# Linear attention and a cos-gated MLP on one core: three subtractions of a row maximum moved from VectorE to GpSimd, with a new order of steps

## The chip, the core and the metric

The kernel runs on one core of a Trainium2 chip. A core has a matrix engine (PE), a vector engine (DVE, also VectorE), a scalar engine (ACT), a general engine (POOL, also GpSimd) and an engine that here only issues transfers (SP); each works through its own list of instructions in order and waits on semaphores for the others. The metric is the device time of one execution in microseconds (us).

## The reference

Eight batches of eight heads, sequence S = 576, head size D = 64, all in float32.

```python
q_s = softmax(q, axis=-1)          # over D, with the row maximum subtracted first
k_s = softmax(k, axis=2)           # over S, with the column maximum subtracted first
kv  = einsum("bhsd,bhse->bhde", k_s, v)
x   = einsum("bhsd,bhde->bhse", q_s, kv)     # to 4608 x 512 (tokens x heads*D)
h   = x @ w_in                     # 512 x 2048
out = (h * cos(h)) @ w_out         # 2048 x 512
```

The subtraction that this document is about is `q - max(q, axis=-1)`, a step of the softmax of q.

## The kernel before, in words

The heads of a batch are taken two at a time; the four pairs of a batch are numbered 0 to 3. A batch's q lies in two tiles of 128 rows by 9 blocks by 128 columns (1152 columns), one for pairs 0 and 1 and one for pairs 2 and 3. Names in the trace: `q`, `qload` (q as loaded; in batch 0, pairs 2 and 3), `qm` (row maxima), `qs` (row sums), `k`, `mt` and `m` (column maxima of k over halves, over all partitions), `kv`, `r`, `kvw` (kv in PSUM, the inverse of its row sums, kv normalised), `qt` (q transposed), `x_False` and `x_True` (the rounded part of q kv, and its remainder), `w_i`, `w_o` (weights of the MLP), `h`, `acc`.

For one tile of q the steps are, each a call of `plan.add` in `q_steps`: the row maximum (`q_max`, DVE, L865), the subtraction (`q_sub`, DVE, L869), the exponential (`q_exp`, ACT, L880 and L883), the row sum (`q_sum`, DVE, L888), its inverse (`q_inv`, DVE, L892 and L893) and the normalisation (`q_norm`, DVE, L896). For k: `k_max` and its two followers (DVE, L698, L703, L707), `k_all`, the maximum over all 128 partitions (POOL, an all-reduce, L713), `k_sub` (DVE, L720), `k_exp` (ACT, L726). Then PE takes `kv` (L775), DVE makes `kvw` (L792, L795, L802), PE transposes q (`qt`, L1013) and multiplies (`x_False`, `x_True`, L1062). In batch 0 each pair of k goes through these steps by itself, in later batches two pairs together. The MLP runs in units of 512 columns of tokens; its first product is `h` at L1233, its second `acc` at L1509. The weights come as raw 512 KB blocks and are split into a rounded part and a remainder by ACT (L502, L507, L528) and DVE (L511, L517, L537), block by block, before the unit that needs them.

All of this is first written down as a list of steps. `plan.add(engine, us, fn, reads, writes)` appends one; the `us` there is a planning number and is not used when the kernel is built. The list `ORDER`, written out as step numbers, then says in which order the steps are issued, and so in which order each engine meets them:

```python
steps = plan.order(ORDER)
for i in steps:
    if plan.steps[i][2]:
        plan.steps[i][2]()
```

Nothing reorders them later: an engine that waits for one step holds up everything behind it on the same engine.

Of the kernel before, what the change touches and what calls it, by code (L numbers as in the profile page):

```python
# [49 lines left out]
    KVD=((0, 0), (0, 1), (0, 2), (0, 3), (1, 0), (1, 1), (1, 2), (1, 3)),  # L50
    SB=3,
# [220 lines left out]
def linear_attention_then_cos_gated_mlp(  # L272
# [203 lines left out]
    def convert(ws, f):  # L476
# [55 lines left out]
        def lo():  # L532
            t = T["wp", ws, f]
            for i, w in enumerate(ws):
                c, h, l = T["wc", ws, f][:, i], t[:, i, 0].bitcast(F32), t[:, i, 1]
                if w == "i":
                    nc.vector.tensor_sub(l, c, h)  # L537
                else:
                    nc.vector.tensor_sub(split(l), dealt(c), split(h))
# [1225 lines left out]
```

## Time and profile before

| | us |
|---|---|
| median of three runs | 812.35 |
| the three runs | 810.69, 812.35, 813.06 |
| the profiled execution, whole | 811.02 |
| its span, first to last instruction | 809.2 |
| PE busy in the span | 789.3 |
| DVE busy | 647.3 |
| ACT busy | 545.9 |
| POOL busy | 42.7 |

The span is what the trace shows; the execution adds 1.8 us around it. A busy time is the sum of an engine's instructions, without its waits. The granted clock of PE was 0.999 of full speed.

### The profile page before, as it was taken

What the parts mean: (1) busy time and instruction counts of PE and PEld (TensorE: products, weight loads), DVE (VectorE), ACT (ScalarE), POOL (GpSimd) and SP (SyncE); (2) the same over time, 40 slices, a digit from 0 to 9 for tenths busy, and PEclk for the clock granted to TensorE, in tenths of its full rate; (3) what the DMA queues carried; (4) which work ended last, traced back from release to release, by engine and by line L of the source; (5) the groups of instructions that cost most, each with busy time, mean ns of one, the idle gap of its engine ahead of it and who ended that gap; (6) DMA issues with size and microseconds to landing.
All of it is one profiled execution on the core that took longest, in us unless ns stands there. A gap on an engine that the chain in (4) does not pass through costs nothing.

```text
span 809.2 us, 14405 instructions
## 1 busy us (share of the span) xinstructions
PE 789.3 (98%) x5172; PEld 707.2 (87%) x5172; DVE 647.3 (80%) x1140; ACT 545.9 (67%) x1004; POOL 42.7 (5%) x153
## 2 busy tenths in 40 slices
PE   3899999999999999999999999999999999999997
PEld 2766888888888889999999999999999999999996
DVE  9999999889789898999787879887797656654444
ACT  4999888955656558767877678676666565555441
POOL 1200100000100010002000110003000000000000
PEclk9999999999999999999999999999999999999999
DMA  7877833458665688889889988897977676546621
GB/s 233 274 220 214 246 117 122 149 154 238 188 194 164 145 255 263 242 259 261 235 273 258 274 273 253 227 286 248 296 203 215 235 255 245 190 174 222 220 80 53
DMA packets 202967, 175.02 MB, mean 216 GB/s; under 512 B 111120, under 2 KB 173072, under 8 KB 202896
## 3 DMA queue, kind: packets, MB, share of 16 engines
q1 hardware_dynamic: 202576, 173.58, 71.0%
q8 instruction: 41, 0.67, 0.3%
q10 hardware_dynamic: 320, 0.52, 0.2%
q14 instruction: 30, 0.25, 0.1%
HBM read 139.72 MB, written 34.34 MB: 215 GB/s over the span
## 4 chain that ended last, share of the span: by engine, by line
PE 97%; SPq 2%; DMA 1%; issue 0%; DVE 0%
PE acc L1509 44%; PE h L1362 20%; PE h L1233 16%; PE pb L1362 8%; PE x_False L1062 3%; PE acc L1502 3%; PE kv L775 2%; DMA v<-in_v_dram 1%; PE x_True L1062 0%; PE qt L1013 0%; SPq L632 0%; SPq L583 0%; SPq L574 0%; SPq L613 0%; SPq L663 0%
## 5 line engine op out<-in xcount | busy, mean ns | idle before, releaser
L1239 ACT ACTIVATE kt<-h 128x512 int32<-128x512 f32 x144 | 85.8, 596 | 112.0 <-PE h L1362 82.8
L1509 PE MATMUL acc<-w_o,ghi 128*128 128x512 f32 x456 | 136.4, 381 | 0.0
L1243 DVE SCALAR_TENSOR_TENSOR kt<-kt,h 128x512 f32<-128x512 int32 x144 | 97.1, 681 | 36.2 <-ACT kt L1239 35.3
L1249 ACT ACTIVATE kt<-kt 128x512 f32<-128x512 f32 x144 | 89.3, 629 | 34.4 <-DVE kt L1243 33.3
L1255 DVE TENSOR_TENSOR kt<-kt,h 128x512 f32<-128x512 f32 x138 | 92.6, 682 | 19.1 <-ACT kt L1249 17.1
L1233 PE MATMUL h<-x,w_i 128*128 128x512 f32 x396 | 92.1, 383 | 0.0
L1509 PE MATMUL acc<-w_o,w_io 128*128 128x512 f32 x360 | 91.4, 379 | 0.0
L1509 PEld LDWEIGHTS acc<-w_o,ghi 128*128 128x128 f32 x456 | 82.2, 190 | 9.5
L1509 PE MATMUL acc<-w_o,glo 128*128 128x512 f32 x228 | 86.4, 379 | 0.0
L1233 PEld LDWEIGHTS h<-x,w_i 128*128 128x128 f32 x396 | 74.1, 189 | 12.2 <-issue 0.7
L1509 PE MATMUL acc<-w_io,ghi 128*128 128x512 f32 x264 | 78.9, 381 | 0.0
L1362 PE MATMUL h<-x,w_i 128*128 128x256 f32 x502 | 75.9, 276 | 0.0
L1362 PEld LDWEIGHTS h<-x,w_i 128*128 128x128 f32 x502 | 69.3, 191 | 3.0 <-DVE h L1388 0.6
L1509 PEld LDWEIGHTS acc<-w_o,w_io 128*128 128x128 f32 x360 | 63.6, 190 | 6.4
L1362 PE MATMUL h<-w_i,w_i 128*128 128x256 f32 x428 | 68.2, 276 | 0.0
L1272 DVE TENSOR_TENSOR glo<-kt,ghi 128x512 fp32r<-128x512 f32 x90 | 61.1, 682 | 8.9 <-ACT ghi L1266 8.6
L1266 ACT CAST ghi<-kt 128x512 fp32r<-128x512 f32 x90 | 55.3, 620 | 18.8 <-DVE kt L1255 10.9
L1362 PEld LDWEIGHTS h<-w_i,w_i 128*128 128x128 f32 x428 | 59.4, 191 | 2.2 <-ACT h L1381 0.2
L1509 PEld LDWEIGHTS acc<-w_io,ghi 128*128 128x128 f32 x264 | 47.0, 190 | 5.2
L1362 PE MATMUL pb<-x,w_i 128*128 128x256 f32 x314 | 50.9, 275 | 0.0
L1509 PE MATMUL acc<-w_io,glo 128*128 128x512 f32 x132 | 50.0, 379 | 0.0
L1509 PEld LDWEIGHTS acc<-w_o,glo 128*128 128x128 f32 x228 | 43.1, 189 | 6.1
(166 smaller groups left out, 1515.6 us busy)
## 6 DMA issues: line engine op xcount, KB each, us to landing
w_i<-combined SPq DMA_DIRECT2D x106, 512.0 KB, 4.8
w_io<-combined SPq DMA_DIRECT2D x55, 512.0 KB, 4.8
out_dram<-o SPq DMA_DIRECT2D x32, 256.0 KB, 3.1
k<-in_k_dram SPq DMA_DIRECT2D x14, 512.0 KB, 4.8
q<-in_q_dram SPq DMA_DIRECT2D x28, 256.0 KB, 4.0
qb<-q_rows SPq DMA_DIRECT2D x96, 72.0 KB, 3.3
q_rows<-q SPq DMA_DIRECT2D x24, 256.0 KB, 2.8
combined<-w_i SPq DMA_DIRECT2D x23, 256.0 KB, 3.0
```

The source lines that it names most:

```text
L775: nc.tensor.matmul(x[h * D : (h + 1) * D, odd : odd + vt.shape[1]], t[:, h, c, :], vt, start=(c == CM), stop=(c == CM - 1),)
L1062: nc.tensor.matmul(t[:, 0:HALF], a, c[:, cs] if whole else woven(c[:, cs]), start=(n == 0), stop=(n == len(parts) - 1 and not again))
L1233: nc.tensor.matmul(o, a, woven(x), start=(c == 0 and n == 0), stop=(c == KC - 1 and n == 2))
L1239: nc.scalar.activation(t, T["h", u], AF.Identity, bias=0.25, scale=1.0 / TWO_PI)
L1243: nc.vector.scalar_tensor_tensor(t.bitcast(F32), t, -TWO_PI, T["h", u], op0=ALU.mult, op1=ALU.add)
L1249: nc.scalar.activation(t, t, AF.Sin, bias=0.5 * math.pi)
L1255: nc.vector.tensor_mul(o, t, T["h", u])
L1266: nc.scalar.copy(t, T["kt", u].bitcast(F32))
L1272: nc.vector.tensor_sub(t, T["kt", u].bitcast(F32), T["gh", u].bitcast(F32))
L1362: nc.tensor.matmul(dst(), w[:, cs], x.rearrange("p a i -> p i a"), start=start and j == 0 and n == 0, stop=j == 1 and n == 2, skip_group_c ...
L1502: nc.tensor.matmul(T["acc", j], T["g", u][:, js], T["wc", "o", f][:, 0], start=first, stop=last)
L1509: nc.tensor.matmul(T["acc", j], a[:, js], woven(w), start=(first and n == 0), stop=(last and n == 2))
```

## The change

A new option names tiles of q by batch, half of the batch's pairs, and part; for the three that it lists, `q_sub` is issued on GpSimd.

```diff
+    GQ=((0, 1, 0), (1, 0, 0), (1, 1, 0)),
...
             def q_sub():
                 x = rows("qraw")
-                nc.vector.tensor_sub(x, x, over_d(T["qm", b, a][:, c0:c1]))
+                e = nc.gpsimd if (b, a, i) in CFG["GQ"] else nc.vector
+                e.tensor_sub(x, x, over_d(T["qm", b, a][:, c0:c1]))
...
-            plan.add("DVE", dve, q_sub, reads=ms, writes=ql)
+            if (b, a, i) in CFG["GQ"]:
+                plan.add("POOL", 2 * dve, q_sub, reads=ms, writes=ql)
+            else:
+                plan.add("DVE", dve, q_sub, reads=ms, writes=ql)
```

The three are pairs 2 and 3 of batch 0, and both halves of batch 1; each instruction is 128 rows by 1152 columns. Six other options come with the diff (`QA`, `ZIG`, `TWX`, `GK`, `GN`, `GW`); they are empty or zero, and with these values the code takes the path that it took before. `ORDER` is replaced as a whole by another order of the same number of steps. In the program that is built, DVE has three instructions fewer and POOL three more; POOL also gets four instructions that exchange the set of GpSimd routines, since a subtraction and an all-reduce belong to different sets. The other instructions are the same, in another order.

On POOL, from the start of batch 0's all-reduces; ISA with operands is an all-reduce, ISA without operands an exchange of the set of routines. In a name such as `m_0_2_336` the first number is the batch, the second the pair, the third a running number. Before:

```order
L713 ISA m_0_0_242<-m1_0_0_233 128x128
L713 ISA m_0_1_261<-m1_0_1_245 128x128
L569 MEMSET k_1_0_297 64x4x64
L713 ISA m_0_2_336<-m1_0_2_319 128x128
L713 ISA m_0_3_394<-m1_0_3_356 128x128
L713 ISA m_1_0_484<-m1_1_0_459 128x128
L569 MEMSET k_1_2_491 64x4x64
L713 ISA m_1_0_484<-m1_1_0_459 128x128
L713 ISA m_1_2_580<-m1_1_2_559 128x128 x2
```

Now (L725 is the all-reduce, L886 the subtraction):

```order
L725 ISA m_0_0_242<-m1_0_0_229 128x128
L725 ISA m_0_1_263<-m1_0_1_247 128x128
L886 ISA
L886 TENSOR_TENSOR qload_0_1_215<-qload_0_1_215,qm_0_1_261 128x1152
L725 ISA
L725 ISA m_0_2_331<-m1_0_2_317 128x128
L581 MEMSET k_1_0_340 64x4x64
L725 ISA m_0_3_381<-m1_0_3_356 128x128
L725 ISA m_1_0_455<-m1_1_0_435 128x128 x2
L581 MEMSET k_1_2_473 64x4x64
L725 ISA m_1_2_546<-m1_1_2_535 128x128 x2
```

The subtraction stands between the all-reduces of pairs 1 and 2 of batch 0, with an exchange of routines ahead of it and another behind it. The two subtractions of batch 1 follow the all-reduces of batch 1 in the same way (an exchange ahead, an exchange behind).

On DVE, from the row sum of batch 0's second tile on. Before:

```order
L888 TENSOR_REDUCE qs_0_1_338<-q_0_1_312 128x18
L802 SCALAR_TENSOR_TENSOR kvw_0_1_352<-kv_0_1_301,r_0_1_333,mask_83 128x128
L703 TENSOR_TENSOR m1_0_3_356<-mt_0_3_325 128x128
L720 TENSOR_TENSOR k_0_2_185<-k_0_2_185,m_0_2_336 128x640
L511 SCALAR_TENSOR_TENSOR wc_sb_175<-raw_i0_205,wc_sb_175 128x512
L892 TENSOR_SCALAR qs_0_1_338<-qs_0_1_338 128x18
L893 RECIPROCAL qs_0_1_338<-qs_0_1_338 128x18
L707 TENSOR_TENSOR m1_0_3_356<-m1_0_3_356,k_0_3_193 128x128
L896 TENSOR_TENSOR q_0_1_312<-q_0_1_312,qs_0_1_338 128x1152
L792 TENSOR_SCALAR r_0_2_397<-kv_0_2_379 128x1
L795 RECIPROCAL r_0_2_397<-r_0_2_397 128x1
L720 TENSOR_TENSOR k_0_3_193<-k_0_3_193,m_0_3_394 128x640
```

Now (L905 is the row sum, L914 the normalisation, L733 the subtraction of k, L546 the remainder of a weight block, L808, L811 and L818 make kvw):

```order
L909 TENSOR_SCALAR qs_0_1_333<-qs_0_1_333 128x18
L910 RECIPROCAL qs_0_1_333<-qs_0_1_333 128x18
L733 TENSOR_TENSOR k_0_2_183<-k_0_2_183,m_0_2_331 128x640
L719 TENSOR_TENSOR m1_0_3_356<-m1_0_3_356,k_0_3_209 128x128
L914 TENSOR_TENSOR q_0_1_313<-q_0_1_313,qs_0_1_333 128x1152
L733 TENSOR_TENSOR k_0_3_209<-k_0_3_209,m_0_3_381 128x640
L710 TENSOR_TENSOR mt_1_0_402<-k_1_0_340 128x512
L546 TENSOR_TENSOR w_i0_326<-wc_sb_175,w_i0_326 128x512
L808 TENSOR_SCALAR r_0_2_432<-kv_0_2_405 128x1
L811 RECIPROCAL r_0_2_432<-r_0_2_432 128x1
L715 TENSOR_TENSOR m1_1_0_435<-mt_1_0_402 128x256
L818 SCALAR_TENSOR_TENSOR kvw_0_2_444<-kv_0_2_405,r_0_2_432,mask_83 128x128
```

The subtraction of pair 2's k, which needs the all-reduce of pair 2, still stands ahead of pair 3's last maximum, of the normalisation of q and of kvw of pair 2; between the subtraction of pair 3's k and kvw of pair 2 there now stand the first maximum of batch 1's k, the remainder of the first weight block and a second maximum. The two steps on the first weight block (L511 and L517 before) have moved to the place that the subtraction of q has left, ahead of the row sum.

On PE, from the first products of pair 1 to the first product of the MLP, without the transposes between them. Before:

```order
L1013 MATMUL qt1_0_2_401<-ident_76,q_0_1_312 128x128 x4
L1017 MATMUL qt2_0_2_406<-ident_76,q_0_1_312 128x128
L1062 MATMUL x0_0_1_True_412<-qt_0_1_327,kvw_0_1_352 128x288
L1067 MATMUL x0_0_1_True_412<-x_0_1_377,neg_81 128x288
L1062 MATMUL x1_0_1_True_421<-qt_0_1_327,kvw_0_1_352 128x288
L1067 MATMUL x1_0_1_True_421<-x_0_1_377,neg_81 128x224
L1013 MATMUL qt1_0_3_426<-ident_76,q_0_1_312 128x128 x4
L1062 MATMUL x0_0_2_False_435<-qt_0_2_415,kvw_0_2_418 128x288
L1062 MATMUL x1_0_2_False_442<-qt_0_2_415,kvw_0_2_418 128x288
L775 MATMUL kv_0_3_445<-v_0_3_195,k_0_3_193 64x66 x2
L775 MATMUL kv_0_3_445<-v_0_3_195,k_0_3_193 64x65 x8
L1233 MATMUL h_0_462<-x_0_0_344,w_i0_433 128x512 x3
```

Now (L791 is kv, L1120 and L1125 make x, L1293 is the first product h):

```order
L1120 MATMUL x1_0_1_True_391<-qt_0_1_335,kvw_0_1_359 128x288
L1125 MATMUL x1_0_1_True_391<-x_0_1_379,neg_81 128x224
L1071 MATMUL qt1_0_2_395<-ident_76,q_0_1_313 128x128 x4
L1075 MATMUL qt2_0_2_400<-ident_76,q_0_1_313 128x128
L791 MATMUL kv_0_2_405<-v_0_2_187,k_0_2_183 64x66 x2
L791 MATMUL kv_0_2_405<-v_0_2_187,k_0_2_183 64x65 x8
L791 MATMUL kv_0_3_421<-v_0_3_193,k_0_3_209 64x66 x2
L791 MATMUL kv_0_3_421<-v_0_3_193,k_0_3_209 64x65 x8
L1071 MATMUL qt1_0_3_438<-ident_76,q_0_1_313 128x128 x4
L1120 MATMUL x0_0_2_False_447<-qt_0_2_418,kvw_0_2_444 128x288
L1120 MATMUL x1_0_2_False_458<-qt_0_2_418,kvw_0_2_444 128x288
L1293 MATMUL h_0_463<-x_0_0_346,w_i0_326 128x512 x3
```

The kv of pairs 2 and 3 now stand together ahead of the transposes of pair 3, and the work ahead of the first h is the same as before.

## Rows read from the trace of the kernel before

**Rows 1.** Page, parts 1 and 4: busy time by engine; the chain that ended last

```profile
PE 789.3 (98%) x5172; PEld 707.2 (87%) x5172; DVE 647.3 (80%) x1140; ACT 545.9 (67%) x1004; POOL 42.7 (5%) x153
...
PE 97%; SPq 2%; DMA 1%; issue 0%; DVE 0%
```

**Rows 2.** Waits of PE: engine, line, awaited, us in total, times, longest us

```profile
PE qt L1013 <- DVE q L896: 11.6, 1, 11.6
PE kv L775 <- DMA v<-in_v_dram: 2.4, 1, 2.4
```

**Rows 3.** Windows: busy us (instructions) by engine, granted PE clock, DMA share, GB/s

```profile
20.00:40.00 20.00, 17.55 (x150) 14.13 (x149) 18.62 (x38) 19.41 (x43) 6.00 (x6) 1.00 0.89 277
```

**Rows 4.** Source line L321: count, ns least/median/most, first and last start

```profile
L321 POOLq MODIFY_POOL_CONFIG  x2: 11/11/11, 1.0 to 1.0; - x2
L321 POOL PARTITION_ALL_REDUCE first<-first x1: 360/360/360, 1.1 to 1.1; - x1
```

**Rows 5.** Timeline of POOL: start us, duration us, instruction, idle before

```profile
12.64 0.70 POOL L713 PARTITION_ALL_REDUCE m<-m  x1 [1.94 <-DVE m L707]
...
21.50 1.73 POOL L713 PARTITION_ALL_REDUCE m<-m  x1 [3.13 <-DVE m L707]
...
37.56 1.76 POOL L713 PARTITION_ALL_REDUCE m<-m  x2 [5.41 <-DVE m L707]
72.61 0.31 POOL L569 MEMSET k<- 64x256 f32 x1 [33.29 <-ACT q L874]
```

**Rows 6.** Groups of POOL by line and shape: busy us, mean ns

```profile
L569 POOL MEMSET k<- 64x256 f32 x14 | 4.3, 307 | 339.9 <-DVE qf L1120 68.7 <-DVE qt L1050 57.0 <-DMA q_rows<-q 55.4
L347 POOL MEMSET v<- 64x132 f32 x20 | 4.1, 203 | 1.2
...
masks.py:199 POOL TENSOR_SCALAR_AFFINE_SELECT ident<-ident 128x128 f32<-128x128 f32 x1 | 0.4, 355 | 0.0
```

**Rows 7.** Timeline of DVE, same columns as the timeline of POOL

```profile
14.46 1.35 DVE L869 TENSOR_TENSOR qload<-qload,qm 128x1152 f32<-128x1152 f32 x1
...
17.75 1.33 DVE L888 TENSOR_REDUCE qs<-q 128x18 f32<-128x1152 f32 x1
...
20.19 0.69 DVE L511 SCALAR_TENSOR_TENSOR wc_sb<-raw_i,wc_sb 128x512 int32<-128x512 int32 x1
...
21.18 0.23 DVE L707 TENSOR_TENSOR m<-m,k 128x128 f32<-128x128 f32 x1
21.32 1.35 DVE L896 TENSOR_TENSOR q<-q,qs 128x1152 f32<-128x1152 f32 x1
23.91 0.22 DVE L792 TENSOR_SCALAR r<-kv 128x1 f32<-128x1 f32 x1 [1.24 <-PE kv L775]
...
24.25 0.81 DVE L720 TENSOR_TENSOR k<-k,m 128x640 f32<-128x640 f32 x1
24.98 0.34 DVE L802 SCALAR_TENSOR_TENSOR kvw<-kv,r,mask 128x128 f32<-128x128 f32 x1
...
26.44 0.68 DVE L698 TENSOR_TENSOR mt<-k 128x512 f32<-128x512 f32 x1
27.04 0.68 DVE L537 TENSOR_TENSOR w_i<-wc_sb,w_i 128x512 fp32r<-128x512 f32 x1
27.64 0.42 DVE L703 TENSOR_TENSOR m<-mt 128x256 f32<-128x256 f32 x1
```

**Rows 8.** Timeline of ACT

```profile
15.84 0.31 ACT L880 ACTIVATE q<-qload 128x128 f32<-128x128 f32 x1 [0.26 <-DVE qload L869]
16.06 1.13 ACT L883 ACTIVATE q<-qload 128x512 f32<-128x512 f32 x2
```

**Rows 9.** Timeline of PE

```profile
26.05 1.14 PE L1062 MATMUL x_False<-qt,kvw 128*128 128x288 f32 x4
...
27.85 0.92 PE L1233 MATMUL h<-x,w_i 128*128 128x512 f32 x3
```

**Rows 10.** DMA issues: count, KB each, median us from issue to landing

```profile
raw_i<-in_moe_w_in_dram SPq DMA_DIRECT2D x11, 512.0 KB, 5.9
```

More of the change, by code (lines that the diff above doesn't have):

```diff
@@ L50 @@
     KVD=((0, 0), (0, 1), (0, 2), (0, 3), (1, 0), (1, 1), (1, 2), (1, 3)),
+    QA={},
+    ZIG=0,
+    TWX=(),
+    GQ=((0, 1, 0), (1, 0, 0), (1, 1, 0)),
+    GK=(),
+    GN=(),
+    GW=(),
     SB=3,
@@ L535, in lo @@
                 c, h, l = T["wc", ws, f][:, i], t[:, i, 0].bitcast(F32), t[:, i, 1]
-                if w == "i":
+                if w == "i" and f in CFG["GW"]:
+                    nc.gpsimd.tensor_sub(l, c, h)
+                elif w == "i":
                     nc.vector.tensor_sub(l, c, h)
@@ L549, in parts @@
             plan.add("ACT", 0.62 * n + dealing, hi, reads=C, writes=R)
-            plan.add("DVE", 0.69 * n + dealing, lo, reads=C, writes=R)
+            if f in CFG["GW"] and ws == "i":
+                plan.add("POOL", 1.38 * n, lambda: lo(), reads=C, writes=R)
+            else:
+                plan.add("DVE", 0.69 * n + dealing, lo, reads=C, writes=R)
         if wait:
@@ L719, in k_sub @@
             t, x = T["k4", b, p0], T["m", b, p0]
-            nc.vector.tensor_sub(
+            e = nc.gpsimd if (b, p0) in CFG["GK"] else nc.vector
+            e.tensor_sub(
                 t, t, x.rearrange("p h (o d) -> p h o d", o=1).broadcast_to([P, nh, NC, D])
@@ L732, in k_exps @@
             plan.add("POOL", 1.05, lambda i=i: k_all(i), reads=[m1], writes=[m])
-        plan.add("DVE", us[3], k_sub, reads=[m], writes=kr)
+        if (b, p0) in CFG["GK"]:
+            plan.add("POOL", 2 * us[3], k_sub, reads=[m], writes=kr)
+        else:
+            plan.add("DVE", us[3], k_sub, reads=[m], writes=kr)
         plan.add("ACT", us[4], k_exp, writes=kr, table="exp")
@@ L895, in q_norm, with q_max_neg, q_rows @@
             def q_norm():
-                nc.vector.tensor_mul(rows(), rows(), over_d(T["qs", b, a][:, c0:c1]))
-            dve, act = 0.15 + 0.1335 * n, 0.22 + 0.105 * n
+                e = nc.gpsimd if (b, a, i) in CFG["GN"] else nc.vector
+                e.tensor_mul(rows(), rows(), over_d(T["qs", b, a][:, c0:c1]))
+            def q_max_neg():
+                nc.vector.tensor_reduce(out=sums("qm"), in_=rows("qraw"), axis=AX.X, op=ALU.max, negate=True)
+            def q_rows(cs):
+                if ("q", b, a) not in T:
+                    T["q", b, a] = sbt([P, 9, P], F32, "kq", f"q_{b}_{a}", place)
+                sums("qs")
+                for c in cs:
+                    for h in range(2):
+                        x = T["qraw", b, a]
+                        d = slice(h * D, (h + 1) * D)
+                        if flat and c:
+                            lo = (c - 1) // CM * CM + 1
+                            x = q_heads(x[:, lo : lo + CM])[:, h, c - lo]
+                        else:
+                            x = x[:, c, d]
+                        more = dict(accum_out=T["qs", b, a][:, c, h : h + 1]) if accum else {}
+                        nc.scalar.activation(
+                            T["q", b, a][:, c, d], x, AF.Exp, bias=T["qm", b, a][:, c, h : h + 1], **more
+                        )
@@ new lines, in part @@
+            dve, act = 0.15 + 0.1335 * n, 0.22 + 0.105 * n
+            accum = CFG["QA"].get((b, a))
+            if accum is not None:
+                plan.add("DVE", dve, q_max_neg, reads=ql, writes=ms, due=due)
+                for c in range(c0, c1, 3):
+                    cs = range(c, min(c + 3, c1))
+                    plan.add(
+                        "ACT", (0.56 + 0.2 * accum) * len(cs), lambda cs=cs: q_rows(cs), reads=ql + ms, writes=qr + ss * accum, table="exp"
+                    )
+                if not accum:
+                    plan.add("DVE", dve, q_sum, reads=qr, writes=ss)
+                plan.add("DVE", 0.44, q_inv, writes=ss)
+                plan.add("DVE", dve, q_norm, reads=ss, writes=qr)
+                return
@@ L899, in part @@
             plan.add("DVE", dve, q_max, reads=ql, writes=ms, due=due)
-            plan.add("DVE", dve, q_sub, reads=ms, writes=ql)
+            if (b, a, i) in CFG["GQ"]:
+                plan.add("POOL", 2 * dve, q_sub, reads=ms, writes=ql)
+            else:
+                plan.add("DVE", dve, q_sub, reads=ms, writes=ql)
             plan.add("ACT", act + (0.22 * (n // CM) - 0.22 * (n == CM) if flat else 0.0), q_exp, reads=ql, writes=qr, table="exp")
@@ L903, in part @@
             plan.add("DVE", 0.44, q_inv, writes=ss)
-            plan.add("DVE", dve, q_norm, reads=ss, writes=qr)
+            if (b, a, i) in CFG["GN"]:
+                plan.add("POOL", 2 * dve, q_norm, reads=ss, writes=qr)
+            else:
+                plan.add("DVE", dve, q_norm, reads=ss, writes=qr)
         if (b, a) in CFG["QP"]:
@@ L1006, in x_steps @@
         cols = [slice(0, HALF), slice(HALF, TB)]
-        twice = b < CFG["PELO"]
+        twice = b < CFG["PELO"] and p not in CFG["TWX"]
         def q_tr():
@@ L1203, in linear_attention_then_cos_gated_mlp @@
     order = []
+    if CFG["ZIG"]:
+        segs = [segs[0], (1, 0, NF), segs[2]]
     for b, f0, f1 in segs + [(b, 0, NF) for b in range(2, B + 1)]:
@@ L1707, in linear_attention_then_cos_gated_mlp @@
                     X[b] = attend(b, (b - 1) * NF, ("att", "att", "att"))
+                    if b == 1 and CFG["ZIG"]:
+                        nth["x4k"] += 4
                 else:
```

322 rows, old and new, of the table ORDER are left out of this document.

## The prediction

> **What bounds the kernel now.** I read the busy times first: PE is busy for 789.3 us of 809.2, and the chain that ended last is 97% PE [rows 1]. So a change can win only where PE stands still. The waits of PE say where that is: 11.6 us for the first normalised q, at the very start, and 2.4 us for the transfer of v at the kv of pair 2 of batch 0 [rows 2]. The windows show the stretch that the change works in: from 20 to 40 us PE is busy for 17.55 of 20, DVE for 18.62 and ACT for 19.41 [rows 3], so there DVE and ACT are as full as PE, and what is put on one of their chains is seen by PE. PE's idle time is 809.2 - 789.3 = 19.9 us in all, and 14.0 of it are the two waits. The reader is to keep from this that the change can win at most some 2.4 us behind the head, while a late step of batch 0 costs its full delay: behind it PE is full to the end, and a full PE gives nothing back.
>
> **The change, part by part.** Three subtractions leave DVE, each as long as the one of batch 0: 1.35 us [rows 7]. Three arrive on GpSimd, with four exchanges of the set of routines. The order of the steps is new. The batch 0 part stands on the path that PE waits for; the batch 1 part is taken after it.
>
> *The subtraction on GpSimd, P.* No row of before shows it. From below: a memset of 256 columns takes 0.307 us [rows 6], and 1152 columns at that rate take 1.4, though a memset reads nothing. From above: the select over 128 columns, which reads one tile and writes one, takes 0.355 us, nine times that is 3.2. The memsets of 256 and 132 columns (0.307 and 0.203, rows 6) leave about 0.1 us fixed, so the select gives (0.355 - 0.1) x 9 + 0.1 = 2.4 us. I take 2.4, since the subtraction reads as the select does; the ends move the sum by -1.0 and +0.8.
>
> *The exchange of routines, S.* The trace has one place of the kind, at the start: two configuration rows of 11 ns at 1.0 us, and the first all-reduce at 1.08, of 0.36 us [rows 4]. So from below an exchange costs 0.1 us. But each execution ends and begins with the same set there, so this row need not hold a load of code. If code must come from memory, the nearest row is a load from DRAM in the same stretch: a raw weight block takes 5.9 us from issue to landing [rows 10]. From above: an exchange has two configuration rows, and two loads one after the other are 11.8 us. I take 5.9, a single load, because the routines must be somewhere, and the row at 1.0 us is the one case in which nothing need be fetched.
>
> The Trainium skill bears on this in "GPSIMD Engine Reference", section 2.1 (Instruction dispatch): the first call to a freshly loaded kernel pays an instruction load of about 6 us (5.95 measured there), with no instruction of its own in the profile. The only such place in the trace, 0.1 us, does not show it; by the page's figure the sum below would be 0.1 us more, by the row's 0.1 us it would be the first rival.
>
> *Batch 0, step by step.* POOL is in order, and the subtraction with its two exchanges stands between the all-reduces of pairs 1 and 2. The all-reduce of pair 1 ends at 12.64 + 0.70 = 13.34 [rows 5]. Exchange, 13.34 + 5.9 = 19.24; subtraction, 21.64. The subtraction of before ended at 14.46 + 1.35 = 15.81 [rows 7], so the exponentials, which took from 15.84 to 16.06 + 1.13 = 17.19 [rows 8], end at about 23.0, and the row sum with its 1.33 us at 24.3 and not at 19.08 [rows 7]. That is one chain. The other, and the longer, is POOL's: the exchange back is done at 21.64 + 5.9 = 27.54, the all-reduce of pair 2 (0.70) at 28.24, and only then can DVE subtract from pair 2's k, 0.81 us, 29.05. Behind that instruction wait, on DVE, the last maximum of pair 3, the normalisation of q and the kvw of pair 2. From the start of that maximum to the end of pair 3's all-reduce before took 21.18 to 21.50 + 1.73 = 23.23, so 2.05 us with the normalisation beside it [rows 5, 7]: 31.10. The subtraction from pair 3's k ends at 31.91. Then, in the new order, a maximum and the weight remainder (0.60 us from start to start, 26.44, 27.04, 27.64 in rows 7), the inverse of kv's sums (23.91 to 24.25: 0.34), a second maximum (0.42) and kvw (0.34): 31.91 + 1.20 + 0.34 + 0.42 + 0.34 = 34.2. PE's x_False of pair 2 takes 1.14 us [rows 9], so the first product of the MLP starts at about 35.35. Before it started at 27.85 [rows 9], with the same PE work ahead of it. The delay is 7.5 us. The transfer of v, 2.4 us, lies inside it and ends earlier, so nothing is taken off for it.
>
> S stands in this chain twice: the delay is 7.5 - 2 x (5.9 - S). Nothing is lost up to S = 2.1, and at S = 3.35 the loss is 2.4 us, 0.3% of the time, which is about what a measurement of this kernel can tell from no change.
>
> *DVE's freed time.* In batch 0 it is 1.35 us, and its place is taken by two weight steps of 0.69 us [rows 7]; they are only moved, so the 1.35 us do come back later. In the forecast DVE waits for POOL in this stretch, and time freed on an engine that waits is nothing.
>
> *Batch 1.* Two exchanges and two subtractions are 2 x 5.9 + 2 x 2.4 = 16.6 us. POOL has the room: between 37.56 + 1.76 = 39.32 and 72.61 it stands idle for 33.29 us [rows 5]. This cover hides them; without it the 16.6 us would stand in q of batch 1. If GpSimd's reading holds DVE up, the two together cost DVE at most 2 x 2.4 less the 2 x 1.35 freed, 2.1 us. That such a hold exists is seen at 21.50: an all-reduce beside DVE's normalisation at 21.32 takes 1.73 us, the one at 12.64 took 0.70 [rows 5, 7]. I take nothing for it, and 2.1 us into the range.
>
> **The sum.** 809.2 + 7.5 = 816.7 us of span, so 818.5 for the profiled execution of 811.02. The median of the runs, 812.35, is 1.3 us above that execution; on it the forecast is 812.35 + 7.5 = 819.9 us. With S between 3.4 and 8.4, as far again on either side of 5.9, it runs from 814.9 to 824.9.
>
> **Rival 1, the exchange is cheap.** If S is below 2.1 us, POOL's chain no longer decides: with 0.1 the subtraction can start at 14.46 at the latest, where DVE's did, and ends 2.4 us later at 16.9, at most 1.1 us behind DVE's. What is left is the new order: DVE has 1.35 us less, and two weight steps have come ahead of the row sum for it. For this speaks the 0.1 us of rows 4. Against it: that row has no need of a load. The time: between -0.5 and +2.4 us, 812 to 814.7, no change that could be told.
>
> **Rival 2, faster.** The exchange is cheap and the two loads of v and k come as early as PE can take them. The place is PE's 2.4 us wait at kv of pair 2 [rows 2]: now pair 1's x_True and the transposes of pair 2 stand ahead of that kv, so the wait can fall away. Where PE waits for DVE behind it, DVE's 1.35 us come on top, so 2.4 to 3.75 us, in the middle 3.1, 809.3. It needs S under 2.1; from there up the POOL chain makes PE wait longer than v did, and the gain is gone. For it speaks that the wait is real and the order goes around it; against it, again, S.
>
> **Rival 3, two loads for an exchange.** S = 11.8: the delay is 7.5 + 2 x 5.9 = 19.3 us, 831.7. For it speak the two configuration rows at one place [rows 4]; against it, that both start within the same 0.1 us, so that they could be one load.
>
> **How the numbers follow.** Forecast (S from 3.4 to 8.4 and its neighbours): 0.60. Rival 1: 0.20. Rival 2: 0.11. Rival 3: 0.09. The prediction is 819.9. The range leaves out rivals 2 and 3, 0.20 together: it begins with rival 1 at 812.0 and ends at 828.0, which is 824.9 with P at its upper end (+0.8) and the hold of batch 1 (+2.1). The forecast's own range is 814.9 to 824.9. Faster by over 0.3%: 0.11, rival 2. Within 0.3%: 0.20, rival 1. Slower: 0.60 + 0.09 = 0.69.
>
> **What would show it.** POOL's timeline: a gap between the end of pair 1's all-reduce and the start of the subtraction, and one between its end and the all-reduce of pair 2. Each should be about 5.9 us; if either is under 2 us the forecast falls, over 9 us rival 3 comes in. The subtraction itself: 2.4 us. DVE's row sum of q should start at about 23.0, its subtraction from pair 2's k at 28.2. PE: the first product of the MLP at about 35.3, and a new wait for DVE or POOL of several us ahead of it in place of the 2.4 us for v. Behind batch 0 PE's waits should be as few as before; if there are new ones around batch 1, the 2.1 us or the cover of POOL were judged wrong. What would make the prediction wrong is above all S: every us of it is two in the sum.

## The result, and the profile after

The changed kernel takes 823.43 us in the median (822.98 to 823.89, four runs) against 812.70 of before (810.69 to 813.86): 10.7 us more. The ratio on record is 1.0145 with an interval of 1.013 to 1.0161; the two medians alone give 1.0132, which lies inside it. It is slower, as was forecast. In the three later comparisons of this study the kernel before was at 811.77, 811.38 and 811.01; 823.43 is 11.7 to 12.4 us above these, so 12 us is the better figure for the loss. The profiled execution has a span of 821.6 us, 12.4 more than before; the granted clock of PE is 0.991 on the mean.

The waits of PE in the changed kernel, to be set beside [rows 2] (L1071 is the transpose, L1125 and L1120 make x_True and x_False, L818 is kvw, L1134 the rounding of x on ACT):

```profile
PE qt L1071 <- DVE q L914: 11.5, 1, 11.5
PE x_True L1125 <- ACT x L1134: 6.6, 1, 6.6
PE x_False L1120 <- DVE kvw L818: 3.6, 1, 3.6
PE kv L791 <- ACT k L739: 1.1, 2, 0.8
```

The head is as it was, 11.5 us. The 2.4 us for v are gone, and 6.6 and 3.6 us have come in their place, for ACT and for DVE. Neither names POOL, and one step further back each leads to it. For ACT that step is on its own timeline: the rounding of x (L1134, 25.07) stands behind the exponentials of q (L897), which waited 7.37 us for POOL's subtraction:

```profile
22.68 0.31 ACT L897 ACTIVATE q<-qload 128x128 f32<-128x128 f32 x1 [7.37 <-POOL qload L886]
...
25.07 0.64 ACT L1134 CAST x<-x_False 128x288 fp32r<-128x288 f32 x2
```

For DVE it is shown further below. The timeline of POOL, beside [rows 5] (start us, duration, instruction, idle time before it):

```profile
12.54 0.71 POOL L725 PARTITION_ALL_REDUCE m<-m  x1 [1.94 <-DVE m L719]
20.54 2.11 POOL L886 TENSOR_TENSOR qload<-qload,qm 128x1152 f32<-128x1152 f32 x1 [7.30 <-issue]
29.52 0.72 POOL L725 PARTITION_ALL_REDUCE m<-m  x1 [6.87 <-issue]
...
32.27 1.65 POOL L725 PARTITION_ALL_REDUCE m<-m  x1 [1.66 <-DVE m L719]
...
44.77 1.88 POOL L725 PARTITION_ALL_REDUCE m<-m  x2 [4.94 <-DVE m L719]
56.19 2.35 POOL L886 TENSOR_TENSOR q<-q,qm 128x1152 f32<-128x1152 f32 x1 [9.54 <-DMA v_sb<-in_v_dram]
```

The all-reduce of pair 1 is done at 13.25, and the subtraction starts at 20.54: 7.29 us. It is done at 22.65, and the next all-reduce starts at 29.52: 6.87 us. What ended these gaps is "issue", so the profile shows no engine that POOL waited for. The instructions by source line show what stands there; here are the rows of the subtraction and of the all-reduce that belong to POOL's own queue (count, least/median/most ns, first and last start):

```profile
L886 POOLq MODIFY_POOL_CONFIG  x4: 88/88/88, 13.1 to 46.6; - x4
```

```profile
L725 POOLq MODIFY_POOL_CONFIG  x4: 1/2/4, 22.9 to 77.0; - x4
```

Two configuration rows of 88 ns at 13.1 us and two more, of 1 to 4 ns, at 22.9; the other four are in batch 1. The row is short; the 7 us stand behind it and have no row of their own. Those at the start of the program before were of 11 ns [rows 4].

In front of the second gap and behind it, on DVE (L905 is the row sum, L715 and L719 a maximum of pair 3's k, L733 the subtraction from k, L914 the normalisation, L808 the first step of the inverse for kvw of pair 2):

```profile
24.06 1.35 DVE L905 TENSOR_REDUCE qs<-q 128x18 f32<-128x1152 f32 x1 [6.43 <-ACT q L900]
30.28 0.29 DVE L715 TENSOR_TENSOR m<-mt 128x128 f32<-128x128 f32 x1 [4.86 <-POOL m L725]
30.49 0.34 DVE L818 SCALAR_TENSOR_TENSOR kvw<-kv,r,mask 128x128 f32<-128x128 f32 x1
...
31.13 0.76 DVE L733 TENSOR_TENSOR k<-k,m 128x640 f32<-128x640 f32 x1
...
32.00 1.35 DVE L914 TENSOR_TENSOR q<-q,qs 128x1152 f32<-128x1152 f32 x1
...
36.53 0.23 DVE L808 TENSOR_SCALAR r<-kv 128x1 f32<-128x1 f32 x1 [0.55 <-PE kv L791]
...
37.19 0.35 DVE L818 SCALAR_TENSOR_TENSOR kvw<-kv,r,mask 128x128 f32<-128x128 f32 x1
```

DVE stands for 6.43 us until the exponentials are there, and for 4.86 us more until POOL's all-reduce is. The instruction that waits in the second case is not the subtraction from pair 2's k but the one at 30.28, four ahead of it; behind it stand kvw of pair 1 (30.49) and with it PE's x_False of pair 1. On PE:

```profile
25.52 0.61 PE L1125 MATMUL x_True<-x,neg 128*128 128x288 f32 x1 [6.57 <-ACT x L1134]
...
30.88 2.29 PE L1120 MATMUL x_False<-qt,kvw 128*128 128x288 f32 x4 [3.61 <-DVE kvw L818]
...
35.68 1.39 PE L791 MATMUL kv<-v,k 128*64 128x66 f32 x40
...
38.45 1.02 PE L1293 MATMUL h<-x,w_i 128*128 128x512 f32 x3
```

The first product of the MLP starts at 38.45, 10.6 us later than before [rows 9]. In the window from 20 to 40 us PE was busy for 10.87 us and its granted clock was 0.66 on the mean, where before it was 17.55 us and 1.00 [rows 3]; the columns are those of [rows 3], and the second row is the stretch in which x_False of pair 1 ran, at 0.50, the lower of the clock's two levels (1.2 of 2.4 GHz):

```profile
20.00:40.00 20.00, 10.87 (x74) 8.29 (x75) 9.83 (x22) 11.11 (x31) 6.61 (x7) 0.66 0.34 97
```

```profile
30.00:33.00 3.00, 2.12 (x5) 1.53 (x6) 2.69 (x7) 0.65 (x2) 1.28 (x3) 0.50 0.00 0
```

### The profile page after: what moved, and what is told of

Its sections match the earlier page's. It is cut to its first block, busy times and chain, and to the rows that moved or that the text cites. A ratio compares the mean times of both kernels' runs of the same rounds, so it can differ in the third digit from the quotient of the medians.

```text
span 821.6 us, 14430 instructions
## 1 busy us (share of the span) xinstructions
PE 793.4 (97%) x5172; PEld 709.8 (86%) x5172; DVE 645.3 (79%) x1137; ACT 545.8 (66%) x1004; POOL 51.3 (6%) x156
## 2 busy tenths in 40 slices
DMA packets 202967, 175.02 MB, mean 213 GB/s; under 512 B 111120, under 2 KB 173072, under 8 KB 202896
## 4 chain that ended last, share of the span: by engine, by line
PE 92%; DVE 2%; ACT 2%; issue 1%; DMA 1%; POOL 1%; SPq 0%; DVEq 0%; POOLq 0%
PE acc L1569 42%; PE h L1422 19%; PE h L1293 15%; PE pb L1422 8%; PE x_False L1120 3%; PE acc L1562 2%; PE kv L791 2%; DMA w_io<-combined 1%; POOL m L725 1%; PE x_True L1120 1%; DMA qload<-in_q_dram 0%; DVE qm L881 0%; ACT L1309 0%; PE qt L1071 0%; POOL qload L886 0%
## 5 line engine op out<-in xcount | busy, mean ns | idle before, releaser
L1293 PE MATMUL h<-x,w_i 128*128 128x512 f32 x396 | 91.8, 384 | 0.0
L1293 PEld LDWEIGHTS h<-x,w_i 128*128 128x128 f32 x396 | 74.6, 189 | 11.8 <-issue 1.0
L1332 DVE TENSOR_TENSOR glo<-kt,ghi 128x512 fp32r<-128x512 f32 x90 | 61.5, 687 | 11.0 <-ACT ghi L1326 10.6
L1441 ACT COPY h<-pb 128x256 f32<-128x256 f32 x96 | 34.3, 363 | 21.4 <-DVE kt L1315 17.6
```

The costliest lines, as they stand in the source:

```text
L1293: nc.tensor.matmul(o, a, woven(x), start=(c == 0 and n == 0), stop=(c == KC - 1 and n == 2))
L1332: nc.vector.tensor_sub(t, T["kt", u].bitcast(F32), T["gh", u].bitcast(F32))
L1441: nc.scalar.copy(half(k, 0), pair(0))
```

## The experiments

**Theory A**: the exchange of the set of routines holds GpSimd for some 7 us each time, and two of them stand in batch 0's chain. **Theory B**: the new order of steps costs. **Theory C**: the subtraction costs by its length on GpSimd, or by holding DVE. All times are medians; each ratio is the one on record (not exactly the quotient of two medians), to runs of the kernel before on the same chip, whose median was 811.77 us for the first four, 811.38 for the next four, 811.01 for the last.

**The new order alone.**

```diff
-    GQ=((0, 1, 0), (1, 0, 0), (1, 1, 0)),
+    GQ=(),
```

> The new order of steps with all three subtractions left on DVE. Theory A: the loss comes from the exchanges of routines around the subtraction of batch 0 (20.54 - 13.25 = 7.29 us before it and 29.52 - 22.65 = 6.87 us behind it in the changed kernel). Then this kernel has no such gap, its first product of the MLP starts near 28 us and not at 38.45, and its time is within 0.3% of the kernel before, 810 to 815 us; at most the some 2 us of small late waits of PE in the changed kernel (at 88, 399, 403 and 546 us) could remain. Theory B: the new order is itself what costs; then this kernel stays near 823 us.

Measured: 815.08 us, ratio 1.0046 (1.0031 to 1.006), just outside the 810 to 815 expected. The all-reduce of pair 2 starts at 18.81 us and not at 29.52, after a wait for DVE, and on PE the first product of the MLP starts at 27.66:

```profile
18.81 0.70 POOL L725 PARTITION_ALL_REDUCE m<-m  x1 [5.50 <-DVE r L808]
```

```profile
27.66 1.02 PE L1293 MATMUL h<-x,w_i 128*128 128x512 f32 x3
```

So theory A holds for the 8 us that are gone. B has a share, though: the order by itself is 0.3 to 0.6% slower than before. Its cost lies behind batch 0: behind the first product PE waits for 3.9 us in all, and the profiled execution of before has no wait there (the kernel with the late exchanges below, in the order of before, has 0.8). The waits for DVE among the 3.9:

```profile
PE h L1422 <- DVE h L1451: 1.1, 1, 1.1
PE h L1293 <- DVE g L1315: 0.6, 1, 0.6
PE acc L1562 <- DVE g L1315: 0.5, 1, 0.5
```

The profiled span is 5.0 us longer than that of before (814.2 against 809.2), so about 1 us is not located.

**The old order with GpSimd.** The changed kernel with `ORDER` of before.

> The order of before with the three subtractions on GpSimd. Theory A: the same two gaps of about 7 us around the subtraction of batch 0, slower than before by 8 to 13 us, 820 to 826 us. Theory B (the order costs): no loss, 811 to 814 us.

Measured: 824.39 us, 1.0157 (1.014 to 1.0174). The order of before is hit as hard. Its gaps on POOL were 7.39 us ahead of the subtraction and 7.81 behind it (the second counted from the end of a memset of 0.31 us that follows the subtraction). The first product starts at 41.02 us, 13.2 later than before; the span is 12.7 us longer, so all of the loss is there by then:

```profile
20.49 2.11 POOL L886 TENSOR_TENSOR qload<-qload,qm 128x1152 f32<-128x1152 f32 x1 [7.39 <-PE x_False L1120]
...
30.77 0.72 POOL L725 PARTITION_ALL_REDUCE m<-m  x1 [7.81 <-issue]
```

**Batch 0 alone, and batch 1 alone.**

```diff
-    GQ=((0, 1, 0), (1, 0, 0), (1, 1, 0)),
+    GQ=((0, 1, 0),),                       # batch 0 alone
+    GQ=((1, 0, 0), (1, 1, 0)),             # batch 1 alone
```

> The changed kernel with only the subtraction of batch 0 on GpSimd, those of batch 1 back on DVE. Theory A: the whole loss stands in batch 0, within 2 us of the changed kernel, 821 to 825 us. Theory C: each subtraction on GpSimd costs by its own length (2.1 to 2.35 us against 1.35) and by holding DVE; then a third of the loss, 815 to 817 us.

> The changed kernel with only the two subtractions of batch 1 on GpSimd. Theory A: the exchanges lie in POOL's idle time, so within 0.3% of the new order alone, 810 to 815 us, and a subtraction starts some 0.2 us after its row maximum, as in the changed kernel (row maximum done at 55.96, subtraction at 56.19). Theory C: two thirds of the loss, 818 to 820 us.

Measured: batch 0 alone 826.20 us, 1.0178 (1.0158 to 1.0198), which is more than with all three; batch 1 alone 813.24 us, 1.0022 (1.0011 to 1.0034), which is less than the order alone. So the loss is batch 0's: 823.43 - 813.24 = 10.2 us in the new order. The expectation for batch 0 alone, 821 to 825, was missed. Of the 2.8 us by which that kernel is behind the changed one (3.2 between the profiled spans), 1.65 are lost before batch 1 counts: its first product starts at 40.10 and not at 38.45. The head's wait was 0.5 us longer there, and the granted clock stayed at 0.50 until 37.4 us, against 34.7 in the changed kernel.

```profile
40.10 1.02 PE L1293 MATMUL h<-x,w_i 128*128 128x512 f32 x3
```

What batch 1 on GpSimd brings is clearer in two waits of PE for DVE, at L1293 and L1562, 1.1 us together: both kernels with batch 1 on DVE have them, and with batch 1 alone on GpSimd they are gone. The medians without batch 0 say 815.08 - 813.24 = 1.8 us, with runs that overlap (814.05 to 817.01 against 810.79 to 815.44). So in the new order the two subtractions of batch 1 are better off on GpSimd, by 1 to 2 us. Their exchanges are hidden:

```profile
45.40 2.35 POOL L886 TENSOR_TENSOR q<-q,qm 128x1152 f32<-128x1152 f32 x1 [9.54 <-DMA raw_o<-in_moe_w_out_dram]
60.77 2.36 POOL L886 TENSOR_TENSOR q<-q,qm 128x1152 f32<-128x1152 f32 x1 [13.03 <-DMA raw_o<-in_moe_w_out_dram]
```

What PE still waits for there, behind the head, is this (the first at 18 us, in batch 0; of the second, 0.8 us near 390 us):

```profile
PE x_False L1120 <- DVE kvw L818: 1.1, 1, 1.1
PE kv L791 <- ACT k L739: 1.1, 2, 0.8
PE qt L1071 <- DVE x L1156: 0.9, 1, 0.9
PE h L1422 <- ACT h L1441: 0.2, 1, 0.2
```

**An exchange without the long subtraction.** Batch 0's subtraction goes back to DVE; one column on GpSimd keeps the exchanges.

```diff
                 e.tensor_sub(x, x, over_d(T["qm", b, a][:, c0:c1]))
+                if (b, a, i) == (0, 1, 0):     # and (0, 1, 0) out of GQ
+                    nc.gpsimd.tensor_sub(warm, ones, ones)
```

> The new order; batch 0's subtraction is on DVE again, and at its place on GpSimd stands a subtraction of one column of a spare tile, so that the two exchanges of routines stay and the long subtraction goes; batch 1 as changed. Theory A (the exchanges cost): POOL's chain loses only the 2.11 us of the subtraction, so of the 10 to 13 us between this kernel with and without the exchanges in batch 0 some 8 to 10 stay: 820 to 823 us. Theory C (the length of the subtraction, or its hold on DVE): 812 to 815 us, as with batch 1 alone on GpSimd (813.24).

Measured: 824.07 us, 1.0152 (1.0132 to 1.0172): all of the loss, without the subtraction. This is somewhat more than the 820 to 823 expected, since the gaps were longer, 7.87 and 8.02 us, by about as much as the subtraction had taken:

```profile
21.19 0.18 POOL L888 TENSOR_TENSOR first<-first 128x1 f32<-128x1 f32 x1 [7.87 <-ACT wc_sb L509]
29.40 0.72 POOL L725 PARTITION_ALL_REDUCE m<-m  x1 [8.02 <-issue]
```

**A long instruction without an exchange.** The select below reads and writes the same tile and leaves out the subtraction of the row maximum.

```diff
+                if (b, a, i) == (0, 1, 0):
+                    y = T["qraw", b, a].rearrange("p c f -> p (c f)")
+                    nc.gpsimd.affine_select(
+                        out=y, in_=y, compare_op=ALU.not_equal, fill=0.0, base=1,
+                        pattern=[[0, 9 * P]], channel_multiplier=0,
+                    )
+                    return
```

> The changed kernel with a select over the same 128 rows by 1152 columns, of the same set of routines as the all-reduces, in place of batch 0's subtraction: the row maximum is then not subtracted there, and no exchange stands in batch 0. Theory A: some 3.2 us on POOL at the select and no gaps of 7 us, so 811 to 815 us. Theory C: a long instruction of GpSimd at this place is enough to lose most of it, 819 to 823 us.

Measured: 812.50 us, 1.0017 (1.0007 to 1.0027). The select takes 2.60 us, longer than the subtraction's 2.11, and the next all-reduce comes as early as with the subtraction on DVE:

```profile
14.63 2.60 POOL L887 TENSOR_SCALAR_AFFINE_SELECT qload<-qload 128x1152 f32<-128x1152 f32 x1 [0.54 <-DVE qm L881]
18.94 0.70 POOL L725 PARTITION_ALL_REDUCE m<-m  x1 [1.71 <-DVE r L808]
```

The first product of the MLP starts at 27.79 us. Theory C is out: the same place, engine and tile, with a longer instruction and no exchange, loses nothing against batch 1 alone on GpSimd (1.0022). The select reads one operand where the subtraction reads two; that the second operand is not the cause is shown by the one-column run above, which loses as much as the changed kernel without the long subtraction.

**Batch 1 alone in the order of before.** `ORDER` of before with `GQ=((1, 0, 0), (1, 1, 0))`.

> The order of before with only the two subtractions of batch 1 on GpSimd. If DVE's 2.7 us in batch 1 are worth something by themselves, as the two runs with and without them in the new order say (813.24 against 815.08), this one is 1 to 2 us faster than before: about 810. If they are worth something only where the new order makes PE wait for DVE around 47 and 63 us, this one is as before, 811 to 813 us, since PE has no wait behind 46 us in it.

Measured: 811.45 us, 1.0002 (0.9989 to 1.0014). In the order of before DVE's 2.7 us in batch 1 bring nothing that can be measured, so what they bring in the new order only mends what that order had cost.

**One step moved in the changed kernel.** In `ORDER`, kvw of pair 1 follows the inverse of its sums at once:

```diff
-142 50 55 85 102 92 ... 62 158 51 199
+142 50 51 55 85 102 92 ... 62 158 199
```

> The changed kernel with one step moved: kvw of pair 1 stands ahead of the row sum on DVE and no longer behind the maximum of pair 3's k, which in the changed kernel waited until 30.28 us for the all-reduce of pair 2 to free the one buffer of m1. If that wait is what made the first product of the MLP later (38.45) than the two exchanges alone explain (about 37.4), the PE work of pair 1 is done before 29 us and the product starts at 37 to 37.5: 821.5 to 822.5 us. If only the exchanges count, no change, 823.4 us.

Measured: 822.68 us, 1.0138 (1.0116 to 1.016), span 821.1 against 821.6: less than the changed kernel by 0.75 us, just outside the 821.5 to 822.5 expected, with intervals that overlap. The product starts at 37.92 and not at 38.45, 0.53 us earlier, where 0.95 to 1.45 were expected. PE now does pair 1's work while the exchange runs, but the chain goes on through the one buffer of m1 (DVE's 30.28 again) and the normalisation of q, for which PE then waits 2.50 us. Behind that wait kv of pairs 2 and 3 took 2.33 us, against 1.39 in the changed kernel; the granted clock was 0.50 from 33.07 to 36.48 us:

```profile
17.79 0.35 DVE L815 SCALAR_TENSOR_TENSOR kvw<-kv,r,mask 128x128 f32<-128x128 f32 x1
...
30.28 0.29 DVE L712 TENSOR_TENSOR m<-mt 128x128 f32<-128x128 f32 x1 [4.97 <-POOL m L722]
...
30.87 0.76 DVE L730 TENSOR_TENSOR k<-k,m 128x640 f32<-128x640 f32 x1
...
31.75 1.35 DVE L911 TENSOR_TENSOR q<-q,qs 128x1152 f32<-128x1152 f32 x1
```

```profile
33.15 1.12 PE L1068 MATMUL qt<-ident,q 128*128 128x128 f32 x4 [2.50 <-DVE q L911]
...
34.41 2.33 PE L788 MATMUL kv<-v,k 128*64 128x66 f32 x40
...
37.92 1.02 PE L1290 MATMUL h<-x,w_i 128*128 128x512 f32 x3
```

**Four exchanges where nobody waits.** The kernel before, with two spare pairs behind GpSimd's last instruction:

```diff
+        for _ in range(2):
+            nc.gpsimd.tensor_sub(warm, ones, ones)
+            nc.gpsimd.partition_all_reduce(warm, ones, P, RED.max)
```

> The kernel before, and behind GpSimd's last all-reduce (near 559 us, when nothing waits for GpSimd any more) twice a subtraction of one column and an all-reduce of one column of a spare tile, so four exchanges of routines with no wait for data. Theory A: each exchange holds GpSimd for 6 to 8.5 us by itself (5.83 to 8.58 us were seen around batch 0's subtraction), seen as four gaps of that length; and since nobody waits, the time is as before, 810 to 813 us. If a gap is a first-use matter of a routine alone, the second pair's gaps are below 1 us.

Measured: 811.65 us, ratio 1.0 (0.9989 to 1.0012). POOL's timeline has the four gaps:

```profile
568.64 0.30 POOL L1733 TENSOR_TENSOR first<-first 128x1 f32<-128x1 f32 x1 [9.08 <-issue]
575.09 0.38 POOL L1734 PARTITION_ALL_REDUCE first<-first  x1 [6.15 <-issue]
585.56 0.18 POOL L1733 TENSOR_TENSOR first<-first 128x1 f32<-128x1 f32 x1 [10.09 <-issue]
592.29 0.38 POOL L1734 PARTITION_ALL_REDUCE first<-first  x1 [6.55 <-issue]
```

9.08, 6.15, 10.09 and 6.55 us: the second pair costs as much as the first, so it is the exchange and not a first use, and its price varies. Two of the four lie outside the 6 to 8.5 us expected.

## Why the prediction was right, point by point

**What bounds the kernel**, and that a late step of batch 0 costs its full delay: right. The first product of the MLP came 10.6 us later, and the span rose by 12.4; nothing of the 10.6 was given back.

**The exchange, S.** The size, taken from the nearest row, a load from DRAM, was somewhat small: 5.9 us forecast, 7.29 and 6.87 measured, together 2.4 more. In the other kernels it was 5.83 to 10.09. That an exchange costs several us and not 0.1 was reasoned; that the load of a 512 KB weight block came so near to it is luck as far as the rows go, since no run shows that an exchange is a load. The pages count the same DMA traffic before and after, 202967 packets and 175.02 MB, so what fills the 7 us stays open. That the loss of batch 0 is this term and no other is shown from both sides, by the exchange without the subtraction (824.07 us) and the long instruction without the exchange (812.50). In the Trainium skill, "GPSIMD Engine Reference", section 2.1 (Instruction dispatch), the figure is 5.95 us; of the exchanges here the two shortest, 5.83 and 6.15, are near it and the longest is 10.09, so for this kernel the measured 7 us decide.

**The subtraction, P**: 2.4 us forecast, 2.11 in batch 0, 2.35 in batch 1. The select that stood for it took 2.60 over 1152 columns.

**Batch 0's chain.** Its first part held: all-reduce of pair 2 done at 30.24 where 28.24 was forecast, and the 2.0 between them are S and P (2.4 - 0.3, less 0.1 for an earlier start). The row sum came at 24.06, where 23.0 was forecast. Two things were not in it. The subtraction from pair 2's k was put right behind the all-reduce and came 0.89 us after it (31.13), since another instruction of DVE, four ahead, had waited for the same all-reduce: pair 3's maximum writes the only buffer of m1, which the all-reduce of pair 2 reads. The order alone does not show such a wait; the number of buffers in the kernel (`m1=1`) does. And kvw of pair 1 stood behind it too, so that PE's work of pair 1, which the forecast had done by then, fell into the chain (kv of pair 2 at 35.68 us), and at 0.50 of the clock, after PE had stood idle: x_False took 2.29 us, where that of pair 2 took 1.14 before [rows 9]. So 38.45 and not 35.35. The last 1.1 us can be read from the rows. The subtraction from pair 2's k ends 1.65 us after the all-reduce (31.13 + 0.76 - 30.24) and not 0.81, so 0.84 are the instructions ahead of it. DVE then waits 0.55 us for kv of pair 2 (36.53), which PE had late. From there to the first product 0.3 us less were needed than forecast. With kvw moved forward 0.45 of the second part went (DVE waited 0.10 us there) and 0.26 of the first, and the first product came 0.53 us earlier. A second buffer of m1 was not tried.

**Time taken by the order behind batch 0.** Forecast: nothing. With batch 1 alone on GpSimd the new order has its first product at 27.67 us, as early as before, and yet a span 2.1 us longer (811.3 against 809.2; the medians differ by 1.5). In the changed kernel itself the span rose by 1.8 us more than the first product did, and PE has waits of 1.7 us together behind batch 0, which the profiled execution of before does not have. This is a term that the sum lacked. The terms then add up: 7.5 forecast, 2.0 by S and P, 1.1 by the chain, 2.1 by the order, 12.7 us against 12.4 in the span. The forecast of 819.9 was low by a third of the loss.

**Batch 1.** That the exchanges are hidden in POOL's idle time was right: the subtraction starts at 56.19, 0.23 us after its row maximum is done (54.61 + 1.35 = 55.96, last section). That GpSimd might hold DVE for 2.1 us did not come: beside the subtraction of 56.19 two steps of the MLP on DVE (56.48) took 1.28 us, as they did in the new order alone (46.95). The row that was to show such a hold, the all-reduce of 1.73 us at 21.50, is a longer instruction of POOL and says nothing of DVE. The freed time won 1 to 2 us in the new order and nothing in the old.

**The rivals.** Rival 1 says 812 to 814.7 us for an exchange that costs nothing, and the select, which stands for this case, took 812.50. Rival 2 was wrong even without an exchange: the 2.4 us wait for v did go in the new order, but a wait of 1.1 us for kvw came, and the first product moved from 27.85 to 27.67, not by 2.4. Rival 3, two loads for one exchange, is out: no exchange came to 11.8 us. (The upper bound of 828.0 is 827.8 by its own terms; nothing hangs on that.)

None of the kernels here beats the kernel before; the old order with batch 1 on GpSimd is level with it.

## What to carry to other kernels

Before an operation is given to GpSimd, look which set of routines it and its neighbours on that engine belong to. An exchange was 6 to 10 us here, against 1.35 us that the step takes on VectorE; it was free where GpSimd had that much idle time on both sides of the step, as in batch 1; the two in batch 0 delayed the first product by 10.6 us. And where one instruction comes late, look which others write a buffer that it still has to read: they wait too, with all that stands behind them.

## What the runs showed of the hardware

An exchange does not wait for the data of the next routine. In batch 1 of the changed kernel the row is at 46.6 us, and the row maximum that the subtraction needs is this one on DVE:

```profile
54.61 1.35 DVE L881 TENSOR_REDUCE qm<-q 128x18 f32<-128x1152 f32 x1
```

It is done at 55.96; the subtraction started at 56.19, and 0.23 us hold no exchange. So the exchange lay in the 9.3 us before, while the engine waited for data, and one that meets its row early enough costs nothing. Where in the 9.3 us it lay the trace does not show. (The transfer of v that the trace names as releaser of 56.19 is not what it waited for last.) The same section of the Trainium skill, "GPSIMD Engine Reference", 2.1, puts the load at the first call. Read as a load that begins once the operands are there, that would have the subtraction start 6 us after 55.96, and the measurement decides against it.

Its length varies: 5.83 us for a way back in the kernel with batch 0 alone, 10.09 near 575 us with spare instructions and no wait for data. In those four late exchanges the way to the subtraction took 9.08 and 10.09 us, the way back 6.15 and 6.55. The shortest one, 5.83 us, lay in a stretch in which the transfers were at 0.27 of their engines' time, its counterpart of 8.58 us in one at 0.96 (columns as in [rows 3]):

```profile
13.74:22.32 8.58, 5.16 (x50) 3.90 (x50) 4.33 (x13) 1.20 (x4) 0.01 (x1) 1.00 0.96 274
24.43:30.26 5.83, 1.75 (x4) 1.08 (x4) 1.35 (x1) 4.66 (x12) 0.00 (x1) 0.50 0.27 83
```

That transfers lengthen it is not shown: the tiny subtraction's way back took 8.02 us at 0.62, and the changed kernel's way there 7.29 at 0.94.
